# Moving the low halves of the first batch from GpSimd to VectorE, and one load up a place in the queue

## The chip, the cores and the metric

The kernel runs on one core of a Trainium2 chip. The metric is the device time of one execution in microseconds (us); lower is better. The kernel before takes 577.38 us, the median of three runs (576.22 to 577.49). The engines of the core are TensorE (PE in the rows; its weight loads are PEld), VectorE (DVE), ScalarE (ACT), GpSimd (POOL) and the sync engine (SP), whose queue issues all the loads.

## The reference

Three layers run one after the other over 4 batches of 576 positions.

```python
def _attn_ref(q, k, v):          # 8 heads of 64: four local, four strided
    scores = np.where(masks, scale * q @ k.T, -1e9)
    return softmax(scores) @ v

def _moe_ref(x, w_theta, w_tok_r, w_tok_i, w_ch):     # x: (4, 576, 512)
    theta = x @ w_theta
    zr, zi = x * np.cos(theta), x * np.sin(theta)
    y = einsum('ts,bsd->btd', w_tok_r, zr) + einsum('ts,bsd->btd', w_tok_i, zi)
    u = x + y
    return u + np.maximum(u @ w_ch, 0.0)

def _moe2_ref(x, w_gate, wq, wk, wv, wo):   # 4 experts, the top 2 are kept
    ...                                      # causal attention per expert, times wo
```

The change touches the first two layers only, and of these what belongs to batch 0, the weights, and the first load for batch 1.

## The kernel before, in words

**High and low halves.** In these two layers each operand of a large product is kept as two tiles: `hi` (the value rounded, written by ScalarE or VectorE) and `lo` (the value minus `hi`). Each product is three matmuls (`mm3`, lines 260 to 262): hi by hi, hi by lo, lo by hi. Four kinds of tiles are split so. `split_w` splits weights (line 104, or line 106 where there is a scale); the token weights `wtk` and the channel weights `wch` come through `load64`, which takes float64 input apart (lines 131 to 138). `split_act` splits the columns of `X` for theta (line 256). `rotate` splits z, the product of x with cosine and sine (line 328). In `split_w` two of three pieces have their `lo` from GpSimd, one (`c % 3 == 1`) from VectorE; in `split_act` and `rotate` the `lo` comes from GpSimd throughout this part of the program.

**The order of work.** Batch 0 goes alone at first: its attention (`attn_pair`, four pairs of heads, two local and two strided), then `theta(0, 0)`, `sines`, `rotate(0, 0)`, `theta(0, 1)`, `rotate(0, 1)`, `tokens(0, 0)` and `tokens(0, 1)` (the matmuls y). From batch 1 on, the attention of the next batch is mixed in. The program text gives priorities; a scheduler in the framework then orders the instructions of each engine by what it expects to be ready, so the diff alone doesn't tell the order.

**What orders the work near the change.** An engine executes its instructions in order. A theta tile or a y tile takes one of two PSUM buffers (`acc`, `bufs=2`), which come free when VectorE has read the theta tile twice (lines 283, 284) or added y to X (line 343). The transposes of x for `rotate` (`xn`, line 305) have one PSUM buffer, free again after VectorE's product (line 315, or 321 and 322). The raw pieces of the float64 weights go through four slots in `X[3]`, so the load of one piece (line 131) waits until VectorE has read the piece four places before (line 136). SP issues all loads in order: a load that waits holds all behind it. The tiles of batch 1's attention lie where batch 0's lay, so their first load waits for the last use there.

Of the kernel before, what the change touches and what calls it, by code (L numbers as in the profile page):

```python
# [19 lines left out]
ALU = mybir.AluOpType  # L20
# [3 lines left out]
B, S, DM, HD, NE = 4, 576, 512, 64, 4  # L24
# [23 lines left out]
def fused_kernel(ctx: ExitStack, tc: tile.TileContext, ql, kl, vl, qs, ks, vs, wth, wtk, wch, wqk, wvg, wo, out):  # L48
    nc = tc.nc

    def f(ap):
        return ap.bitcast(F32)
# [48 lines left out]
    def split_w(hi, lo, st, scale=1.0, eng=nc.gpsimd):  # L101
        nc.scalar.activation(hi, st, AF.Copy, scale=scale)
        if scale == 1.0:
            eng.tensor_tensor(lo, st, f(hi), op=ALU.subtract)
        else:
            nc.vector.scalar_tensor_tensor(lo, st, scale, f(hi), op0=ALU.mult, op1=ALU.subtract)
# [13 lines left out]
    def load64(dst, src, kt, n0, n1, scale=1.0):  # L120

        hi, lo = dst
        n = n1 - n0
        for c in range(kt):
            raw = X[3].bitcast(U16)[:, c % 4, :4 * n]
            st = X[2][:, c % 4, HALF:HALF + n]  # L130
            nc.sync.dma_start(raw[:, :4 * n - 1], src[:, c, n0:n1].bitcast(U16)[:, 1:])
            mid = raw.bitcast(U32).rearrange("p (n t) -> p n t", t=2)[:, :, 0]
            top = raw.bitcast(BF16).rearrange("p (n t) -> p n t", t=4)[:, :, 2]
            head = X[2][:, c % 4, :n]
            got = nc.scalar.copy(head.bitcast(F16).rearrange("p (n t) -> p n t", t=2)[:, :, 1], top)
            nc.vector.scalar_tensor_tensor(st.bitcast(U32), mid, 13, head.bitcast(U32), op0=ALU.logical_shift_right,
                                           op1=ALU.bitwise_or)
            split_w(hi[:, c, n0:n1], lo[:, c, n0:n1], st, scale, nc.vector if c % 3 == 1 else nc.gpsimd)
        return got.ins

    def per_tile(b, pair, g):
# [106 lines left out]
    def split_act(x, name):  # L248
        hi = act.tile([128, S], F32R, tag="ahi", name=f"{name}_hi")
        lo = act.tile([128, S], F32R, tag="alo", name=f"{name}_lo")  # L250
        if len(xsplit) == B:
            nc.scalar.copy(hi, x)
        else:
            nc.vector.tensor_copy(hi, x)  # L254
        eng = nc.vector if len(xsplit) == B and name.endswith(("0", "2")) else nc.gpsimd
        eng.tensor_tensor(lo, x, f(hi), op=ALU.subtract)  # L256
        return hi, lo

# [5 lines left out]
    def split_x(b):  # L264
        return [split_act(X[b][:, c, :], f"x{len(xsplit)}_{b}_{c}") for c in range(4)]

    sins, turns = {}, {}
    xsplit, trig, z = {}, {}, {}
# [31 lines left out]
    def rotate(b, h):  # L300
        for t in range(NT):
            w, t0, cs = TW[t], 128 * t, trig[h, t]
            xn = ps1.tile([128, 512], F32, tag="xn", bufs=1, name=f"xn_{b}_{h}_{t}")
            for c in range(2):
                nc.tensor.transpose(xn[:w, 128 * c:128 * c + 128], X[b][:, 2 * h + c, t0:t0 + w], ident)
            if t < 4:
                zf = cs
                if h == 0:
                    hi = zu.tile([128, S], F32R, tag="zuhi", name=f"zhi_{b}_{h}_{t}")
                    lo = zu.tile([128, S], F32R, tag="zulo", name=f"zlo_{b}_{h}_{t}")  # L310
                else:
                    hi = z1.tile([128, 512], F32R, tag=f"zhi{t}", name=f"zhi_{b}_{h}_{t}")
                    lo = z1.tile([128, 512], F32R, tag=f"zlo{t}", name=f"zlo_{b}_{h}_{t}")
                hi, lo = (v[:, :512].rearrange("p (a c) -> p a c", a=2) for v in (hi, lo))
                nc.vector.tensor_tensor(zf, cs, xn[:, None, :256].to_broadcast([128, 2, 256]), op=ALU.mult)
                z[h, t], z[h, 4 + t] = (hi[:, 0, :], lo[:, 0, :]), (hi[:, 1, :], lo[:, 1, :])
            else:
                zf = cs[:, 0, :]
                hi = zu.tile([128, 256], F32R, tag="z8hi", bufs=2, name=f"zhi_{b}_{h}_{t}")
                lo = zu.tile([128, 256], F32R, tag="z8lo", bufs=2, name=f"zlo_{b}_{h}_{t}")  # L320
                nc.vector.tensor_tensor(zf[0:64], xn[:64, :256], cs[:64, 0, :], op=ALU.mult)
                nc.vector.tensor_tensor(zf[64:128], xn[:64, :256], cs[:64, 1, :], op=ALU.mult)
                z[h, 8] = (hi, lo)
            if t % 2 == 0 and b > 0:
                nc.vector.tensor_copy(hi, zf)  # L325
            else:
                turns[b, h] = nc.scalar.copy(hi, zf).ins
            nc.gpsimd.tensor_tensor(lo, zf, f(hi), op=ALU.subtract)  # L328

    us = {}  # L330

# [57 lines left out]
    ain = pha.enter_context(tc.tile_pool(name="ain", bufs=3, side="right"))  # L389
# [8 lines left out]
    for b in range(B):  # L398
        angles = theta(b, 0)
        if b > 0:  # L400
            next_pair(b, 0)
            channels(b - 1)
        else:
            sines(b, 0, angles, load64(wtk_s, wtk, 9, 0, HALF))
            load_pair(1, 0, ain, 2, 2)
        rotate(b, 0)
        if b > 0:
            next_pair(b, 1)
# [375 lines left out]
```

## Time and profile before

| | us |
|---|---|
| median of 3 runs | 577.38 |
| lowest, highest | 576.22, 577.49 |
| the profiled execution: its time | 577.79 |
| the profiled execution: its span, first to last instruction | 576.0 |
| TensorE busy in the span | 535.8 (93%) |
| VectorE busy | 404.9 (70%) |
| ScalarE busy | 319.1 (55%) |
| GpSimd busy | 229.6 (40%) |

The span is 1.8 us shorter than the execution's time; that rest lies around the instructions. "Busy" counts the time in which at least one instruction of the engine executes. Matmuls are pipelined and their ends are modelled. The profile names a tile without its buffer number, and the line of the helper that issued the instruction. A row's "idle before" is the time in which the engine did nothing, with the instruction that ended the wait.

### The profile page before, as it was taken

The page shows a single profiled execution, that of the slowest core. Times are in us where ns is not written, and L with a number is a line of the kernel's source. Part 1 is how long each engine was busy: PE and PEld are TensorE (multiplying, and loading weights), DVE is VectorE, ACT ScalarE, POOL GpSimd, SP SyncE. Part 2 cuts the span into 40 slices and gives each one's busy share as a digit, 9 for nine tenths or more (in the row PEclk, how much of TensorE's full clock was granted, in tenths as well). Part 3 has the DMA queues.
Part 4 walks back from the last instruction along what each step waited for, and adds up shares of the span by engine and source line. Part 5 has one row for each costly group of instructions (what it writes and reads, how often), then busy time and mean ns, then how long its engine had stood idle before and what let it go on. Part 6 is the DMA issues. An engine that isn't in the chain of part 4 may idle for free.

```text
span 576.0 us, 12486 instructions
## 1 busy us (share of the span) xinstructions
PE 535.8 (93%) x4536; PEld 512.1 (89%) x4536; DVE 404.9 (70%) x1178; ACT 319.1 (55%) x906; POOL 229.6 (40%) x317
## 2 busy tenths in 40 slices
PE   6847879799999999999999999998999999999987
PEld 5737768799999999999999999887989999999987
DVE  4892796957686647767446553489998898888882
ACT  4882779422636216344233541267678767867873
POOL 3371283622154401355103461345444624644451
PEclk9956999799999999999999999999999999999999
DMA  9667453232320113100100010100001100100012
GB/s 279 230 212 205 136 181 107 69 96 74 105 85 22 64 32 127 33 22 23 56 1 1 1 38 19 38 2 0 2 2 52 34 1 32 42 13 12 32 42 83
DMA packets 20388, 37.52 MB, mean 65 GB/s; under 512 B 2904, under 2 KB 12296, under 8 KB 20328
## 3 DMA queue, kind: packets, MB, share of 16 engines
q1 hardware_dynamic: 20328, 36.73, 20.1%
q8 instruction: 36, 0.59, 0.4%
q14 instruction: 24, 0.20, 0.1%
HBM read 32.01 MB, written 4.72 MB: 64 GB/s over the span
## 4 chain that ended last, share of the span: by engine, by line
PE 65%; DVE 12%; ACT 6%; issue 2%; POOL 1%; POOLq 0%; DVEq 0%; ACTq 0%
PE y L260 6%; PE y L262 6%; PE y L261 6%; PE s L185 3%; PE g L262 3%; PE g L261 3%; PE g L260 3%; PE tp L616 3%; PE th L260 2%; PE av L238 2%; PE th L262 2%; PE th L261 2%; DVE nm L595 2%; PE o L572 2%; PE s L590 2%; PE pq L260 2%
## 5 line engine op out<-in xcount | busy, mean ns | idle before, releaser
L260 PE MATMUL y<-wtk_hi,zhi 128*128 128x288 f32 x288 | 86.9, 302 | 1.9 <-DVE cs L284 1.5
L262 PE MATMUL y<-wtk_hi,zlo 128*128 128x288 f32 x288 | 86.5, 301 | 0.0
L261 PE MATMUL y<-wtk_lo,zhi 128*128 128x288 f32 x288 | 86.3, 300 | 0.0
L328 POOL TENSOR_TENSOR zlo<-cs,zhi 128x512 fp32r<-128x512 f32 (+1 forms) x40 | 47.8, 1205 | 73.8 <-DVE zhi L325 44.2
L212 POOL TENSOR_TENSOR p<-p,sm 128x288 f32<-128x288 f32 (+2 forms) x48 | 29.4, 618 | 97.6 <-DVE sm L211 67.1
L613 POOL TENSOR_SCALAR p<-p,sm,gt 128x256 f32<-128x256 f32 (+1 forms) x64 | 45.3, 710 | 52.1 <-DVE sm L611 33.2
L606 ACT ACTIVATE p<-s,nm 128x128 f32<-128x128 f32 (+2 forms) x96 | 49.6, 518 | 15.0 <-DVE nm L595 7.8
L260 PEld LDWEIGHTS y<-wtk_hi,zhi 128*128 128x128 f32 x288 | 54.9, 191 | 2.5 <-DVE cs L284 1.7
L261 PEld LDWEIGHTS y<-wtk_lo,zhi 128*128 128x128 f32 x288 | 54.8, 190 | 0.2
L262 PEld LDWEIGHTS y<-wtk_hi,zlo 128*128 128x128 f32 x288 | 54.7, 190 | 0.2
L256 POOL TENSOR_TENSOR x_lo<-X,x_hi 128x576 fp32r<-128x576 f32 x24 | 36.9, 1541 | 40.8 <-DVE x_hi L254 34.4
L260 PE MATMUL th<-wth_hi,x_hi 128*128 128x256 f32 (+1 forms) x160 | 48.8, 305 | 3.2 <-ACT X L245 1.7
L185 PE MATMUL s<-k,q 128*108 128x54 f32 (+2 forms) x320 | 45.0, 286 | 4.6 <-DMA k<-in_kl 4.5
L185 PEld LDWEIGHTS s<-k,q 128*108 128x108 f32 (+1 forms) x320 | 43.0, 207 | 6.2 <-issue 6.1
L595 DVE TENSOR_REDUCE nm<-s 128x1 f32<-128x128 f32 (+2 forms) x96 | 44.3, 469 | 5.4 <-PE s L593 4.4
L261 PE MATMUL th<-wth_lo,x_hi 128*128 128x256 f32 (+1 forms) x160 | 46.6, 291 | 0.0
L262 PE MATMUL th<-wth_hi,x_lo 128*128 128x256 f32 (+1 forms) x160 | 46.5, 291 | 0.0
L260 PE MATMUL pq<-x_hi,wqk_hi 128*128 128x288 f32 x128 | 39.8, 311 | 1.0 <-DVE q L541 0.7
L285 ACT ACTIVATE cs<-cs 128x256 f32<-128x256 f32 (+1 forms) x40 | 16.7, 418 | 42.2 <-DVE cs L284 38.6
L260 PE MATMUL g<-u_hi,wch_hi 128*128 128x288 f32 x128 | 38.8, 303 | 0.0
L625 DVE TENSOR_TENSOR ptlo<-tp,pthi 128x128 fp32r<-128x128 f32 (+4 forms) x80 | 37.6, 479 | 1.2 <-ACT pthi L624 0.6
L219 ACT COPY pt<-tp 96x384 f32<-96x384 f32 (+2 forms) x44 | 20.9, 477 | 31.4 <-PE tp L215 31.3
(173 smaller groups left out, 1741.9 us busy)
## 6 DMA issues: line engine op xcount, KB each, us to landing
X<-in_wtk SPq DMA_DIRECT2D x18, 287.8 KB
q<-in_qs SPq DMA_DIRECT2D x8, 594.0 KB
q<-in_ql SPq DMA_DIRECT2D x8, 576.0 KB
v<-in_vl SPq DMA_DIRECT2D x24, 144.0 KB
out_t<-X SPq DMA_DIRECT2D x20, 128.0 KB
k<-in_kl SPq DMA_DIRECT2D x8, 304.0 KB
k<-in_ks SPq DMA_DIRECT2D x8, 288.0 KB
X<-in_wth SPq DMA_DIRECT2D x8, 255.8 KB
```

The source lines that it names most:

```text
L185: nc.tensor.matmul(s[:rm, i * kw:i * kw + w], qt[:, j0 + i, :], kt[:, k0:k0 + w], start=False, stop=i == n - 1)
L212: nc.gpsimd.tensor_tensor(tiles(p), tiles(p), each(sm), op=ALU.mult)
L219: copy(pt[:kw, :n * rm], tp[:kw, :n * rm])
L256: eng.tensor_tensor(lo, x, f(hi), op=ALU.subtract)
L260: nc.tensor.matmul(ps, ahi, bhi, start=first, stop=False)
L261: nc.tensor.matmul(ps, ahi, blo, start=False, stop=False)
L262: nc.tensor.matmul(ps, alo, bhi, start=False, stop=last)
L328: nc.gpsimd.tensor_tensor(lo, zf, f(hi), op=ALU.subtract)
L595: nc.vector.tensor_reduce(nm[:w, t + ci:t + ci + 1], s[:w, :c1 - c0], axis=AX.X, op=ALU.max, negate=True)
L606: nc.scalar.activation(p[:w, c0:c1], scs[ci][:w, :c1 - c0], AF.Exp, bias=nm[:w, t:t + 1], scale=1.0, accum_out=acc)
L613: eng.tensor_scalar(p[:w, :kn], p[:w, :kn], sm[:w, t:t + 1], gt[:w, t, e:e + 1], op0=ALU.mult, op1=ALU.mult)
L625: nc.vector.tensor_tensor(dst(ptlo), src, f(dst(pthi)), op=ALU.subtract)
```

## The change

The low halves that GpSimd computed for the weights `wtk` and `wch`, for the columns of x of batch 0 and for z of batch 0 are computed by VectorE. The first pair of batch 1's attention is asked for before the token weights instead of behind them. Below `rotate` all line numbers grow by one: line 328 before is line 329 after, 343 is 344.

```diff
@@ load64
-            split_w(hi[:, c, n0:n1], lo[:, c, n0:n1], st, scale, nc.vector if c % 3 == 1 else nc.gpsimd)
+            split_w(hi[:, c, n0:n1], lo[:, c, n0:n1], st, scale, nc.vector)
@@ split_act
-        eng = nc.vector if len(xsplit) == B and name.endswith(("0", "2")) else nc.gpsimd
+        eng = nc.vector if not xsplit or len(xsplit) == B and name.endswith(("0", "2")) else nc.gpsimd
         eng.tensor_tensor(lo, x, f(hi), op=ALU.subtract)
@@ rotate
-            nc.gpsimd.tensor_tensor(lo, zf, f(hi), op=ALU.subtract)
+            eng = nc.gpsimd if b > 0 else nc.vector
+            eng.tensor_tensor(lo, zf, f(hi), op=ALU.subtract)
@@ for b in range(B), the branch of b == 0
+            load_pair(1, 0, ain, 2, 2)
             sines(b, 0, angles, load64(wtk_s, wtk, 9, 0, HALF))
-            load_pair(1, 0, ain, 2, 2)
```

`not xsplit` holds only while no batch has been split, so for batch 0's first split. In instructions: 32 subtractions leave GpSimd for VectorE, 4 of x (128x576), 12 of `wtk` (128x288), 6 of `wch` (128x256), 8 of z (128x512) and 2 of z (128x256).

VectorE, from the products of `rotate(0, 0)` to the second tile of `theta(0, 1)` (`cs` holds the angles, then z; `xn` x transposed):

```order
 L136 SCALAR_TENSOR_TENSOR X_63<-X_64,X_63 128x288 x2
+L329 TENSOR_TENSOR zlo_0_0_771<-cs_0_0_630,zhi_0_0_770 128x512
 L315 TENSOR_TENSOR cs_0_3_681<-cs_0_3_681,xn_0_3_791 128x512
 L206 TENSOR_TENSOR p_1_2_1135<-s_1_2_1128,mx_1_2_1133 128x288
+L329 TENSOR_TENSOR zlo_0_1_779<-cs_0_1_647,zhi_0_1_778 128x512
 L283 TENSOR_SCALAR cs_1_0_821<-th_1_0_808 128x256
+L104 TENSOR_TENSOR wtk_lo<-X_63,wtk_hi 128x288
 L243 COPY X_62<-av_0_0_1053 128x384
 L104 TENSOR_TENSOR wtk_lo<-X_63,wtk_hi 128x288
 L321 TENSOR_TENSOR cs_0_4_698<-xn_0_4_799,cs_0_4_698 64x256
+L329 TENSOR_TENSOR zlo_0_2_787<-cs_0_2_664,zhi_0_2_786 128x512
```

The low halves of z and of `wtk` now stand between VectorE's reads of the theta tiles, which free TensorE's PSUM buffers.

TensorE, at the end of `theta(0, 1)` and the start of `tokens(0, 0)` (`tp`, `s`, `av` are attention of batch 1, `y` the token matmuls):

```order
 L262 MATMUL th_1_4_876<-wth_hi,x_0_3_lo 64x256
-L215 MATMUL tp_1_0_1101<-ident,p_1_0_1092 96x128 x3
+L181 LDWEIGHTS twice_89
+L181 MATMUL s_2_2_1397<-mask_s,twice_89 108x162
+L185 MATMUL s_2_2_1397<-k_2_1340,q_2_1339 108x54 x2
+L185 MATMUL s_2_2_1397<-k_2_1340,q_2_1339 108x36
+L215 MATMUL tp_1_2_1143<-ident,p_1_2_1135 96x128 x3
+L238 MATMUL av_1_0_1149<-pt_1_0_1105,v_1_0_1079 64x64 x6
+L238 MATMUL av_1_0_1149<-pt_1_1_1126,v_1_1_1081 64x64 x6
 L260 MATMUL y_0_0_1171<-wtk_hi,zhi_0_0_770 128x288
 L261 MATMUL y_0_0_1171<-wtk_lo,zhi_0_0_770 128x288
```

Attention of batch 1 that stood between the matmuls y, or behind them, now stands before the first of them.

SP, before the change, from the token weights to the first pair of batch 1 (`q_0`, `k_0`, `v_0_0`):

```order
L131 DMA X_64<-in_wtk 128x1151 x13
L157 DMA q_0_757<-in_ql 128x1152
L158 DMA k_0_758<-in_kl 128x608
L162 DMA v_0_0_761<-in_vl 96x384
L162 DMA v_0_1_763<-in_vl 96x384
L162 DMA v_0_2_765<-in_vl 96x384
L157 DMA q_1_1075<-in_ql 128x1152
```

And the same place after the change:

```order
L131 DMA X_64<-in_wtk 128x1151 x12
L157 DMA q_0_702<-in_ql 128x1152
L158 DMA k_0_703<-in_kl 128x608
L162 DMA v_0_0_706<-in_vl 96x384
L162 DMA v_0_1_708<-in_vl 96x384
L162 DMA v_0_2_710<-in_vl 96x384
L131 DMA X_64<-in_wtk 128x1151
L157 DMA q_1_1075<-in_ql 128x1152
```

One piece of the token weights of thirteen has gone behind the pair; the other twelve still stand in front. From the last tiles of `tokens(0, 1)` to the end of the program the order on every engine is what it was.

## Rows read from the trace of the kernel before

**Rows 1.** The page: TensorE's busy tenths in 40 slices of 14.4 us.
```profile
PE   6847879799999999999999999998999999999987
```
**Rows 2.** Busy time by stretch: us, then PE, PEld, DVE, ACT, POOL (instructions), PEclk, DMA share, GB/s.
```profile
65.11:85.13 20.02, 13.31 (x122) 11.65 (x120) 18.76 (x42) 17.26 (x50) 12.95 (x14) 0.91 0.57 181
85.13:107.39 22.26, 18.21 (x161) 17.25 (x161) 16.75 (x29) 16.66 (x44) 10.77 (x13) 1.00 0.24 74
107.39:114.70 7.31, 7.31 (x38) 7.20 (x39) 6.99 (x14) 3.58 (x11) 4.38 (x4) 0.53 0.40 126
133.60:330.00 196.40, 196.31 (x1797) 191.38 (x1796) 124.73 (x314) 81.27 (x179) 61.83 (x61) 1.00 0.14 46
```
**Rows 3.** Timeline of TensorE: start, us, instruction, idle time before it and its releaser.
```profile
52.82 0.43 PE L185 MATMUL s<-k,q 128*128 128x96 f32 x2 [2.75 <-DMA k<-in_kl]
...
70.28 0.69 PE L305 MATMUL xn<-ident,X 128*128 128x128 f32 x2 [2.33 <-DVE cs L315]
...
75.49 0.41 PE L305 MATMUL xn<-ident,X 128*128 128x128 f32 x2 [0.97 <-DVE cs L322]
...
85.13 0.40 PE L260 MATMUL y<-wtk_hi,zhi 128*128 128x288 f32 x1 [1.49 <-DVE cs L284]
...
100.24 0.44 PE L305 MATMUL xn<-ident,X 128*128 128x128 f32 x2 [0.93 <-DVE cs L315]
...
107.39 0.41 PE L305 MATMUL xn<-ident,X 128*64 128x128 f32 x2 [3.12 <-DVE cs L315]
```
**Rows 4.** Timeline of VectorE at 85 us and around 100 us.
```profile
85.00 1.64 DVE L136 SCALAR_TENSOR_TENSOR X<-X,X 128x288 uint32<-128x288 uint32 x1
...
99.52 0.66 DVE L315 TENSOR_TENSOR cs<-cs,xn 128x512 f32<-128x512 f32 x1
100.10 4.80 DVE L136 SCALAR_TENSOR_TENSOR X<-X,X 128x256 uint32<-128x256 uint32 x2
...
106.65 0.68 DVE L315 TENSOR_TENSOR cs<-cs,xn 128x512 f32<-128x512 f32 x1
```
**Rows 5.** Timeline of GpSimd around 100 us.
```profile
99.32 1.28 POOL L328 TENSOR_TENSOR zlo<-cs,zhi 128x512 fp32r<-128x512 f32 x1
100.55 0.74 POOL L212 TENSOR_TENSOR p<-p,sm 108x216 f32<-108x216 f32 x1
101.25 1.44 POOL L104 TENSOR_TENSOR wch_lo<-X,wch_hi 128x256 fp32r<-128x256 f32 x2
102.65 1.29 POOL L328 TENSOR_TENSOR zlo<-cs,zhi 128x512 fp32r<-128x512 f32 x1
103.89 0.72 POOL L104 TENSOR_TENSOR wch_lo<-X,wch_hi 128x256 fp32r<-128x256 f32 x1
```
**Rows 6.** Single lines, whole program: duration in ns, least/median/greatest, first and last start.
```profile
L136 DVE SCALAR_TENSOR_TENSOR X<-X,X x34: 394/450/4087, 20.5 to 106.3; 128x288 uint32<-128x288 uint32 x18, 128x256 uint32<-128x256 uint32 x16
L104 DVE TENSOR_TENSOR wtk_lo<-X,wtk_hi x6: 436/851/1036, 36.0 to 86.6; 128x288 fp32r<-128x288 f32 x6
L256 DVE TENSOR_TENSOR x_lo<-X,x_hi x8: 752/1367/1581, 319.5 to 497.0; 128x576 fp32r<-128x576 f32 x8
```
**Rows 7.** VectorE's groups in 65.11 to 85.13: count, busy us, mean ns, idle before.
```profile
L136 DVE SCALAR_TENSOR_TENSOR X<-X,X 128x288 uint32<-128x288 uint32 x9 | 8.3, 935 | 1.1 <-ACT X L135 1.1
L104 DVE TENSOR_TENSOR wtk_lo<-X,wtk_hi 128x288 fp32r<-128x288 f32 x2 | 1.8, 901 | 0.0
L206 DVE TENSOR_TENSOR p<-s,mx 128x288 f32<-128x288 f32 x2 | 0.9, 452 | 0.1
L254 DVE CAST x_hi<-X 128x576 fp32r<-128x576 f32 x1 | 0.8, 752 | 0.0
```
**Rows 8.** SP's queue: issue of the token weights and of the first pair.
```profile
27.15 15.89 SPq L131 DMA_DIRECT2D X<-in_wtk  x13
43.13 0.38 SPq L157 DMA_DIRECT2D q<-in_ql  x1
```
**Rows 9.** The loads while TensorE waits for k: the stretch, then the size of one piece (page).
```profile
43.13:52.82 9.69, 6.26 (x28) 5.90 (x29) 2.50 (x5) 1.05 (x4) 2.44 (x3) 0.66 0.94 258
X<-in_wtk SPq DMA_DIRECT2D x18, 287.8 KB
```

## The prediction

> **What bounds the kernel now.** I read the page's slices first: TensorE is at nine tenths from the ninth slice on, with dips only before and at the end [rows 1]. Then the busy time by stretch: from 133.6 to 330 us TensorE works 196.31 of 196.40 us [rows 2]. There nothing but its own work counts, and the order of all engines is unchanged. So the change is worth what it does to the time at which TensorE gets there, and that shift is then carried to the end. Between 65 and 107 us TensorE has room: it works 13.31 of 20.02 us and 18.21 of 22.26 us, while VectorE is busy 18.76 of the 20.02 [rows 2]. The timeline of TensorE says for whom it waits [rows 3]: once for the load of k (2.75 us at 52.82), else for VectorE's reads of theta tiles and its products in `rotate`, 0.93 to 3.12 us each.
>
> The longest of these is the lever. At 107.39 TensorE had waited 3.12 us for a product on VectorE that started at 106.65 [rows 3, 4]. VectorE was late because two reads of raw weights (line 136), which start at 100.10, took 4.80 us together [rows 4]. Line 136 has a median of 0.450 us; one of the two is the 4.087 of its range [rows 6]. Meanwhile GpSimd ran low halves and one scaling of p without a gap, from 99.32 to 104.61 [rows 5]. It is no better before: the nine reads in 65.11 to 85.13 have a mean of 0.935 us, twice the median [rows 7]. So VectorE's operations with two inputs in SBUF stand still while GpSimd works. The Trainium skill has this as a lock: SBUF — State Buffer, "Who interferes with whom", says that such an instruction contends with a GpSimd instruction that reads SBUF, and that the loser is blocked for the whole of the other's instruction. By that a VectorE instruction would lose one GpSimd instruction, at most 1.29 us here; the row shows that it can lose several in turn, and the measurement decides. With the rule's single instruction the 3.12 us would have been some other wait and the gain below about half.
>
> **The 32 subtractions.** By rows they cost VectorE, undisturbed: x 0.752 us (the least of line 256 there); `wtk` 0.436, taken as 0.44 (the least of line 104) [rows 6]. For z no row exists on VectorE: 512 columns lie between these two, 0.67 by the columns of x; 0.39 for the half-size ones, the least of line 136. The other end for each is what contended ones cost now: 0.851 for `wtk`, 1.367 for x (medians). I take the low end, since GpSimd, the cause of the high one, is nearly empty in these stretches after the change. It keeps only the scalings of p (0.74) and x of batch 1.
>
> *Up to the first theta.* Four x and six `wtk` add 4 × 0.75 + 6 × 0.44 = 5.6 us to VectorE, and take away GpSimd's share of its stalls of about that size. The transposes that start theta hang on p, scaled on GpSimd behind x halves that are now gone. I count this stretch as nothing, from -1 to +1.
>
> *The load of k.* SP moves one `wtk` piece of 287.8 KB behind the pair, not the token weights as a whole. At the 258 GB/s of the stretch that is 1.1 us [rows 9]. The queue also reaches q without waiting for VectorE to free the thirteenth slot. Thirteen issues take 15.89 us, 1.2 each [rows 8]; I take half of one, 0.6, since q also needs the last attention matmul of batch 0. So **-1.8 us** (0 to -2.75, where the wait is gone and TensorE's own work is next). The moved `wtk` piece belongs to the second half, wanted only behind the sines, so its delay is hidden; if not, ScalarE's read of it and z's high halves behind it are late.
>
> *65 to 85 us, the wait for the first y.* VectorE's read of the fourth theta tile ends this stretch. In the new order there stand ahead of it, more than now: four z (2.7 us) and a half-size one (0.4), seven more `wtk` (3.1), most of the ninth line 136 (0.3), one line 206 (0.45), while the cast of line 254 (0.75) goes behind: 6.2 us. Starts lie 0.08 closer than durations (0.66 us long, 0.58 to the next start [rows 4]); thirteen of these make it 5.2. Away goes the overtime: the nine line 136 have (0.935 - 0.45) × 9 = 4.4 [rows 7], of which the last, 1.64 long from 85.00 [rows 4], has 1.2 behind the point, so 3.2; two line 104 (0.901 - 0.44) × 2 = 0.9. That is 5.2 - 4.1 = 1.1, plus 0.9 for a z that waits on ScalarE and for collisions with p: **+2.0 us** (-1 to +6, the latter with the thirteen at contended durations less what stalls they have now).
>
> *Attention ahead of y.* One transposition, a score tile and the values of pair 1 that ran between or behind the matmuls y now run before the first. TensorE's total is the same and TensorE is in front of a wait there, so y starts later but has less between: 0.
>
> *85 to 115 us.* With GpSimd free of `wch` and z, the 4.80 us become 0.9. VectorE gets six `wch` and five z, about 5.5 us, but loses the stalls, 3.9 there alone, and it has longer than that: the four y tiles take TensorE some 12 us (108 matmuls at the 18.21 us / 161 of this stretch [rows 2]). So both waits, 0.93 and 3.12, go. So does what follows: after the long wait the granted clock is 0.53, that is the lower level (1.2 GHz), for 7.31 us in which TensorE works throughout [rows 2]. At the upper level (2.4 GHz) this work is 7.31 × 0.53 = 3.9 us; 3.4 are lost. Together **-7.45 us** (-9 to -3).
>
> *What is late next.* VectorE adds y to X, frees the PSUM buffer, and in the new order that stands behind `wch` and z. I put 0.5 us on the fourth y and 0.8 on the fifth, which needs the last z: **+1.3 us** (0 to 3). And the clock can fall elsewhere: a wait of 2.33 us at 70.28 was followed by transposes of 0.69 instead of 0.41 us [rows 3]. The new wait before the fifth theta tile is about as long. An even chance of half of 3.4 us: **+0.9 us** (0 to 3.4).
>
> **The sum** goes against the profiled execution, 577.79 us (span 576.0 and 1.8 around it), 0.4 above the median of 577.38: 577.8 - 1.8 + 2.0 - 7.45 + 1.3 + 0.9 = 572.75. I predict 572.8.
>
> **Rivals.**
>
> *VectorE becomes the bound (slower).* In 65 to 85 us it is busy 94%, and the change gives it more. Against: a good part of that is standing still. If the stalls have another cause than GpSimd's low halves, the fourteen added rows cost their contended time, 0.9 us for `wtk` and 1.2 for z, 12.9 us in all with no overtime saved. Then 577.8 - 1.8 + 12.9 - 7.45 = 581.5; with part of the attention hidden in it, 580.5. It decides from the point at which the added rows cost 0.8 us each on average instead of 0.45: then +2.0 becomes +7. The skill's page Perfetto Trace Analysis, "Optimizing Scalar/DVE Operations", speaks for this one: with a saturated VectorE it would move work off it, even to GpSimd. It adds that the two share a port, so that a move between them may not help. By the first half the time is the 580.5; the stalls in the trace bear out the second.
>
> *The long wait moves.* The gap at 104 to 107 is closed, but TensorE then waits 3 us before the fifth theta tile, the clock falls and y starts at the lower level: 3.4 + 2 us back, with the pair of batch 1 still held by bandwidth half of the 1.8: 577.8 - 7.45 + 2.0 + 1.3 + 3.4 - 0.9 = 576.2. For it speaks VectorE's row in 65 to 85; against it that TensorE has some attention to do in between.
>
> *All stalls gone.* GpSimd is so empty that VectorE's stretch breaks even (0 in place of +2.0), k lands in time (-2.75), no clock is lost and the new waits are small (+0.7): 577.8 - 2.75 - 7.45 + 0.7 = 568.3; with GpSimd's p in the way, 569.5.
>
> *The load does nothing*, since twelve pieces still stand in front: 572.8 + 1.8 = 574.6, within the forecast's own range.
>
> **How the numbers follow.** Forecast 0.52 (own range 570.8 to 575.4), long wait moves 0.20 (575.4 to 578), all stalls gone 0.16, slower 0.12. The measurement can't tell 0.2%, 1.15 us, from no change: 576.2 to 578.5. Faster: 0.52 + 0.16 + half of 0.20 = 0.78; same 0.10; slower 0.12. The range from 568.5 to 577.8 leaves out the slower case, a little of the moved wait and the best of the good case, some 0.18.
>
> **What would show it.** VectorE's line 136 and line 104 at 0.45 us before 107 us, with none over 1.5; x and z halves at 0.75 and 0.67; TensorE's wait for k at about 1 us; the first y at 86 to 89; no wait over 1 us and no granted clock under 0.9 from there to 120; the first theta of batch 1, now at 133.6, at about 128.5. Wrong it would be if lines 104 and 329 take 0.8 us and more on VectorE, if y starts behind 91, or if a stretch at the lower clock stands somewhere between 75 and 110.

## The result, and the profile after

The changed kernel takes 569.47 us, the median of 4 runs (567.6 to 571.74), against 576.8 (573.04 to 577.49) for four runs of the kernel before. The ratio is 0.9876, 95% interval 0.984 to 0.991: 7.3 us faster. On a second chip it was 566.59 against 576.9, ratio 0.9846 (0.978 to 0.991). The ratios, here and below, come from the single runs and not from dividing two medians; they leave out runs in the chip's slower state, and the second trace of the changed kernel below is of such a run (574.33 us). The profiled execution takes 568.58 us (span 566.8), 9.2 less than that of before.

TensorE's busy tenths and granted clock in 40 slices, from the page of the changed kernel, against [rows 1]:

```profile
PE   6859689999999999999999999998999999999987
PEclk9958879899999999999999999999999999999999
```

The timeline of TensorE after, at the points that split the span (start, us, instruction, idle time before it and its releaser), against [rows 3]:

```profile
42.46 0.58 PE L260 MATMUL th<-wth_hi,x_hi 128*128 128x256 f32 x1 [1.13 <-ACT X L245]
...
48.69 1.55 PE L185 MATMUL s<-k,q 128*128 128x96 f32 x12 [1.13 <-DMA k<-in_kl]
...
64.56 0.44 PE L305 MATMUL xn<-ident,X 128*128 128x128 f32 x2 [2.33 <-DVE cs L315]
...
83.89 0.40 PE L260 MATMUL y<-wtk_hi,zhi 128*128 128x288 f32 x1
...
105.72 0.28 PE L181 MATMUL s<-mask_s,twice 128*108 128x162 bf16 x1 [0.33 <-DVE p L206]
...
124.32 0.28 PE L260 MATMUL th<-wth_hi,x_hi 128*128 128x256 f32 x1
```

What counts is what is missing: from the first y at 83.89 to the second batch's theta at 124.32 the longest wait is 0.33 us, where 0.93 and 3.12 stood. The 2.33 us of waiting for a product of `rotate` are there as before; the wait for k is 1.13 instead of 2.75.

Busy time by stretch after (us, then PE, PEld, DVE, ACT, POOL, PEclk, DMA share, GB/s), against [rows 2]:

```profile
48.69:83.89 35.20, 28.68 (x249) 26.25 (x249) 29.60 (x84) 26.46 (x79) 5.71 (x8) 0.85 0.54 168
64.56:76.60 12.04, 9.93 (x76) 8.83 (x77) 11.58 (x32) 10.18 (x29) 0.00 (x0) 0.58 0.68 202
83.89:105.72 21.83, 21.50 (x206) 20.90 (x202) 17.72 (x46) 18.00 (x48) 2.80 (x4) 1.00 0.31 104
105.72:109.10 3.38, 3.38 (x29) 3.29 (x30) 2.57 (x10) 1.35 (x7) 1.09 (x2) 0.74 0.63 188
125.00:322.00 197.00, 196.91 (x1801) 191.97 (x1800) 125.01 (x315) 81.24 (x179) 61.85 (x61) 1.00 0.14 46
```

From 125 us on TensorE works throughout again, so what is won by then is carried to the end: the second batch's theta starts 9.27 us earlier (133.59 before) and the span is 9.2 shorter.

VectorE's lines after (ns, least/median/greatest), against [rows 6]; its nine reads of raw weights between 59.40 and 81.83 us (count, busy us, mean ns, idle before), against [rows 7]; and its reads around 96 us, against [rows 4]:

```profile
L136 DVE SCALAR_TENSOR_TENSOR X<-X,X x34: 407/444/915, 20.1 to 97.4; 128x288 uint32<-128x288 uint32 x18, 128x256 uint32<-128x256 uint32 x16
L104 DVE TENSOR_TENSOR wtk_lo<-X,wtk_hi x18: 422/448/708, 36.2 to 81.1; 128x288 fp32r<-128x288 f32 x18
L329 DVE TENSOR_TENSOR zlo<-cs,zhi x10: 415/684/692, 65.2 to 105.0; 128x512 fp32r<-128x512 f32 x8, 128x256 fp32r<-128x256 f32 x2
```

```profile
L136 DVE SCALAR_TENSOR_TENSOR X<-X,X 128x288 uint32<-128x288 uint32 x9 | 4.4, 502 | 1.1 <-ACT X L135 1.1
```

```profile
92.48 1.29 DVE L329 TENSOR_TENSOR zlo<-cs,zhi 128x512 fp32r<-128x512 f32 x2 [0.19 <-ACT zhi L327]
...
96.14 1.65 DVE L136 SCALAR_TENSOR_TENSOR X<-X,X 128x256 uint32<-128x256 uint32 x4
```

The nine reads take 4.4 us where they took 8.3, and four of the later ones 1.65 us where two took 4.80. GpSimd has these rows around that place, against the run without a gap in [rows 5]:

```profile
83.72 1.12 POOL L212 TENSOR_TENSOR p<-p,sm 108x216 f32<-108x216 f32 x2
87.70 1.44 POOL L256 TENSOR_TENSOR x_lo<-X,x_hi 128x576 fp32r<-128x576 f32 x1 [2.86 <-DVE x_hi L254]
96.04 0.46 POOL L212 TENSOR_TENSOR p<-p,sm 108x162 f32<-108x162 f32 x1 [6.91 <-PE y L262]
```

SP's queue after, against [rows 8]: twelve pieces in front of q.

```profile
26.23 14.41 SPq L131 DMA_DIRECT2D X<-in_wtk  x12
41.43 0.33 SPq L157 DMA_DIRECT2D q<-in_ql  x1
```

### The profile page after: what moved, and what is told of

It reads as the page before. It is cut to its first block, busy times and chain, and to the rows that moved or that the text cites. A ratio compares the mean times of both kernels' runs of the same rounds, so it can differ in the third digit from the quotient of the medians.

```text
span 566.8 us, 12483 instructions
## 1 busy us (share of the span) xinstructions
PE 534.0 (94%) x4536; PEld 510.2 (90%) x4536; DVE 401.9 (71%) x1210; ACT 318.2 (56%) x906; POOL 194.9 (34%) x285
## 4 chain that ended last, share of the span: by engine, by line
PE 64%; DVE 12%; ACT 4%; issue 1%; POOL 1%; POOLq 0%; DVEq 0%
PE y L260 6%; PE y L262 6%; PE y L261 6%; PE g L262 3%; PE g L261 3%; PE g L260 3%; PE s L185 3%; PE tp L617 3%; PE th L260 3%; DVE nm L596 2%; PE th L262 2%; PE th L261 2%; PE av L238 2%; PE s L591 2%; PE o L573 2%; PE tp L215 2%
## 5 line engine op out<-in xcount | busy, mean ns | idle before, releaser
L329 POOL TENSOR_TENSOR zlo<-cs,zhi 128x512 fp32r<-128x512 f32 (+1 forms) x30 | 35.8, 1205 | 55.2 <-DVE zhi L325 44.2
L256 POOL TENSOR_TENSOR x_lo<-X,x_hi 128x576 fp32r<-128x576 f32 x20 | 29.6, 1483 | 44.2 <-DVE x_hi L254 37.5
L285 ACT ACTIVATE cs<-cs 128x256 f32<-128x256 f32 (+1 forms) x40 | 16.7, 417 | 38.9 <-DVE cs L284 35.4
```

The lines of the kernel that those rows point to most:

```text
L329: eng.tensor_tensor(lo, zf, f(hi), op=ALU.subtract)
```

## The experiments

Each kernel ran beside the kernel before on the same chip. Four starts on TensorE's timeline split every trace: first theta, the first scores with the newly loaded k, first y, the second batch's first theta. In us:

| kernel | median | ratio to before (95%) | theta starts | to k's scores | to first y | to next theta | theta to theta |
|---|---|---|---|---|---|---|---|
| before | 576.8 | | 43.82 | 9.00 | 32.31 | 48.46 | 89.77 |
| before, second trace | 577.05 | | 43.74 | 7.96 | 32.33 | 47.52 | 87.81 |
| load alone | 577.41 | 1.0005 (0.997 to 1.004) | 42.55 | 8.65 | 34.16 | 47.53 | 90.34 |
| changed | 569.47 | 0.9876 (0.984 to 0.991) | 42.46 | 6.23 | 35.20 | 40.43 | 81.86 |
| changed, second trace | 566.59 | 0.9846 (0.978 to 0.991) | 45.09 | 7.32 | 35.19 | 38.87 | 81.38 |
| halves alone | 566.94 | 0.9866 (0.980 to 0.993) | 41.09 | 7.18 | 35.15 | 38.88 | 81.21 |
| z back | 569.36 | 0.9873 (0.984 to 0.990) | 43.45 | 6.58 | 31.83 | 43.63 | 82.04 |
| weights back | 574.03 | 0.9944 (0.991 to 0.998) | 44.17 | 7.06 | 32.46 | 44.41 | 83.93 |
| x back | 573.07 | 0.9938 (0.991 to 0.996) | 43.18 | 8.22 | 36.66 | 39.80 | 84.68 |
| GpSimd reads | 585.86 | 1.0117 (1.007 to 1.017) | 45.40 | 6.81 | 39.32 | 49.04 | 95.17 |
| GpSimd writes | 568.72 | 0.9853 (0.982 to 0.989) | 42.41 | 6.63 | 32.76 | 41.10 | 80.49 |
| nine pieces behind k | 568.03 | 0.9886 (0.984 to 0.993) | 37.71 | 5.30 | 41.03 | 37.62 | 83.95 |
| five pieces behind k | 571.5 | 0.9918 (0.989 to 0.995) | 39.59 | 5.92 | 34.19 | 42.71 | 82.82 |
| second half behind k | 567.73 | 0.9833 (0.979 to 0.988) | 41.75 | 6.20 | 32.02 | 40.91 | 79.13 |

The start of theta varies by 4 us between traces with one order of instructions (41.09, 42.46, 45.09), so "theta to theta" compares better than the span. The medians are of all runs, and the last four columns are of one trace each.

### Which part brings it: the load or the halves

The load alone, everything else as before:

```diff
+            load_pair(1, 0, ain, 2, 2)
             sines(b, 0, angles, load64(wtk_s, wtk, 9, 0, HALF))
-            load_pair(1, 0, ain, 2, 2)
```

> The kernel before with the pair's load moved alone; every low half stays where it was. Theory 1 (the load moves k, and the clock rises earlier because TensorE's gap is shorter): TensorE's wait for k falls from 2.75 to 1.0-1.6 us, theta then runs at the upper level about 10 us earlier, the first product of rotate comes at 60.5-61.5 instead of 65.11, and the pair of two-input reads that stood 4.8 us at 100 is still there; the time falls by 3 to 4 us, to about 573. Rival A (as the prediction had it: the wait only): first product at 63.3, time 1.8 us down, about 575. Rival B (the early gain of the changed kernel comes from the low halves that leave GpSimd, and the twelve pieces still hold the load back): first product at 64.5-65.1, time within 0.5 us of before.

Measured: no change. The order of instructions is that of the kernel before on every engine; only tile numbers differ, and one group of attention matmuls on TensorE is a place further back. The first product of `rotate` stands at 64.84 us. SP's queue in this kernel:

```profile
25.74 16.04 SPq L131 DMA_DIRECT2D X<-in_wtk  x13
41.87 0.38 SPq L157 DMA_DIRECT2D q<-in_ql  x1
```

Thirteen pieces stand in front of q, as before. VectorE in the same kernel still has its long read:

```profile
100.32 4.79 DVE L136 SCALAR_TENSOR_TENSOR X<-X,X 128x256 uint32<-128x256 uint32 x2
```

Rival B held; theory 1, which I had formed from the result, fell.

The halves alone are the changed kernel with the two load lines in their old order.

> The changed kernel with the pair's load back behind the token weights; all low halves of the first batch stay on VectorE. Theory 1: theta still starts about 1.4 us earlier (42.4), the wait for k grows back to 2.5-3 us or more and the low clock stays until about 55; the long read at 100 and the 3.12 us before the fifth tile of the second half are gone; time about 5 us below before, 572 to 573. Rival B (the halves bring the early gain too): first product at 60.0 or before, time within 1.5 us of the changed kernel, 569.5 to 571. Rival C (gain of the halves given back without the load, VectorE the bound): 575 or more.

Measured: all of the gain. This order is the changed kernel's on every engine; twelve pieces stand in front of q here too. So the load's edit did nothing, and it is the low halves that put the thirteenth piece behind the pair. Rival B came true in time (566.94, beside 566.59 for the changed kernel on that chip) and in place: the first product of `rotate` stands at 58.97. The wait for k was 2.27, less than theory 1's 2.5 to 3, and the lower clock did not last until 55.

Second traces of both kernels, unaltered:

> The kernel before unaltered, for a second trace. If the long read at 100 us is a rule of this order of instructions, one read of raw weights of over 3 us stands there again and TensorE waits about 3 us at 107; if it is chance, the reads there take under 1.5 us and the time is 573 to 574, as the lowest of the runs of before has it (573.04).

> The changed kernel unaltered, for a second trace and for a comparison on the same chip: 569.5 us, -7.3 against before; if the stretches repeat, theta starts at 42.5, the first y at 83.9 and the second batch's first theta at 124.3, each within 0.5 us.

The long read stands in all three traces of this order (before, its second trace, the load alone), so it isn't chance. VectorE and then TensorE in the second trace of before:

```profile
98.99 4.80 DVE L136 SCALAR_TENSOR_TENSOR X<-X,X 128x256 uint32<-128x256 uint32 x2
```

```profile
106.27 0.41 PE L305 MATMUL xn<-ident,X 128*64 128x128 f32 x2 [3.11 <-DVE cs L315]
```

The changed kernel's starts did not repeat within 0.5 us (theta began 2.6 us later); its stretches behind k's scores did (35.20 and 35.19, 40.43 and 38.87; the halves alone have 35.15 and 38.88), but for a piece at the lower clock in the first trace (105.72 above).

### What makes VectorE stand still

Both kernels are the changed one, with GpSimd work added at each of the 32 places from which a low half was taken. Nothing reads its results; what stands behind it on GpSimd, the scaling of p among it, comes later. The calls themselves and the arguments at `[...]` are left out here. The copy of one column in the second kernel ties the fillings to their place, and is the one small read in it.

```diff
+    def extra(hi, lo):                      # reads
+        nc.gpsimd.tensor_tensor(junk[...], f(hi), f(lo), op=ALU.subtract)
...
+    def extra(hi, lo):                      # writes
+        nc.gpsimd.tensor_copy(junk[:, :1], f(lo[...]))
+        for _ in range(2):
+            nc.gpsimd.memset(junk[...], 0.0)
```

> The changed kernel, and GpSimd makes in addition one subtraction of two inputs in SBUF for each of the 32 low parts that it used to make (same widths, x at 512 columns), into a tile that nobody reads; nothing waits for it but what stands behind it on GpSimd (scaling of p, x of the second batch). Theory P: VectorE has all its rows and stands still beside GpSimd as before the change: line 136 at a mean of 0.7 or more between 20 and 115 us, one read of over 2 us at 95 to 103, TensorE's wait for a product of rotate over 1.5 us again; time 6 to 14 us above the changed kernel, 573 to 581. Rival Q (the gain was GpSimd's queue: results come late, p waits behind them): line 136 stays at 0.46 to 0.5 with none over 1.2, TensorE's waits for p grow by 1 to 3 us, time 568 to 570, the same as with writes only.

> As the run with 32 additional subtractions, but GpSimd writes only: at each of the 32 places one copy of a single column, which ties it to the place, and two fillings of the same width with zero. Theory P: VectorE's line 136 stays at 0.46 to 0.5, none over 1.2, no wait over 1 us for a product of rotate in the second half; only what waits for p behind the fillings is later: time 0 to 2.5 us above the changed kernel, 566.6 to 569. Rival W (any work of GpSimd slows VectorE): line 136 at 0.7 or more and the time within 2 us of the run with subtractions.

Measured 585.86 and 568.72. The page's busy times and VectorE's groups between 20 and 115 us (count, busy us, mean ns, idle before), first with reads (145 is line 136, 113 is line 104, 342 is line 329 and 328 is line 315):

```profile
PE 547.4 (93%) x4536; PEld 521.2 (89%) x4536; DVE 410.9 (70%) x1210; ACT 321.9 (55%) x906; POOL 231.7 (40%) x317
...
L145 DVE SCALAR_TENSOR_TENSOR X<-X,X 128x288 uint32<-128x288 uint32 (+1 forms) x34 | 17.8, 550 | 0.8 <-ACT X L144 0.6
L113 DVE TENSOR_TENSOR wtk_lo<-X,wtk_hi 128x288 fp32r<-128x288 f32 x18 | 10.3, 599 | 0.0
L113 DVE TENSOR_TENSOR wch_lo<-X,wch_hi 128x256 fp32r<-128x256 f32 x8 | 6.0, 782 | 0.0
L342 DVE TENSOR_TENSOR zlo<-cs,zhi 128x512 fp32r<-128x512 f32 x8 | 6.4, 806 | 1.0 <-ACT zhi L340 1.0
L328 DVE TENSOR_TENSOR cs<-cs,xn 128x512 f32<-128x512 f32 x8 | 5.5, 682 | 6.1 <-ACT cs L311 4.2 <-PE xn L318 1.8
```

and with writes (144, 112, 341 and 327 are the same lines):

```profile
PE 534.6 (94%) x4536; PEld 509.9 (90%) x4536; DVE 400.7 (71%) x1210; ACT 319.5 (56%) x906; POOL 232.0 (41%) x381
...
L144 DVE SCALAR_TENSOR_TENSOR X<-X,X 128x288 uint32<-128x288 uint32 (+1 forms) x34 | 14.9, 458 | 2.8 <-ACT X L143 2.7
L112 DVE TENSOR_TENSOR wtk_lo<-X,wtk_hi 128x288 fp32r<-128x288 f32 x18 | 8.2, 470 | 0.7 <-ACT wtk_hi L110 0.7
L112 DVE TENSOR_TENSOR wch_lo<-X,wch_hi 128x256 fp32r<-128x256 f32 x8 | 3.2, 418 | 0.0
L341 DVE TENSOR_TENSOR zlo<-cs,zhi 128x512 fp32r<-128x512 f32 x8 | 5.4, 688 | 0.3 <-ACT zhi L339 0.2
L327 DVE TENSOR_TENSOR cs<-cs,xn 128x512 f32<-128x512 f32 x8 | 5.5, 686 | 4.4 <-ACT cs L310 3.6 <-PE xn L317 0.8
```

GpSimd is busy for the same time in both, 231.7 and 232.0 us; VectorE has the same 1210 instructions and needs 10.2 us more beside the reads. Its rows with two inputs in SBUF grow (`wch` from 0.418 to 0.782 us, z from 0.688 to 0.806), and the product of `rotate`, whose xn lies in PSUM so that only one input comes from SBUF, doesn't (0.686 and 0.682). So it is GpSimd's reading that costs, not its being busy, and not its queue: rivals Q and W fall.

How the 10.2 us become the difference in time is less clear. The scheduler ordered VectorE's rows differently in the two kernels, and TensorE is busy 547.4 against 534.6 us with the same 4536 matmuls, since its mean granted clock falls (0.944 and 0.971): part of the price is the clock behind the waits. Neither kernel has the changed one's order on TensorE: 216 and 215 matmuls stand between k's scores and the first y, where the changed kernel has 249.

Of theory P three things missed. Line 136 has a mean of 0.55, not 0.7 or more; the rows of `wtk` and `wch` have 0.60 and 0.78 us instead, which I put down to the additional rows running just behind a low half. No read took over 2 us: the longest has 1.45, so a row that loses several of GpSimd's in turn, as in [rows 4], is seen in the order of before alone. And the time of 585.86 is past the 581 expected at most. TensorE waits 3.42 us for a theta tile in that trace, where a wait for a product of `rotate` had been named.

The Trainium skill, SBUF — State Buffer, "Who interferes with whom", says that a VectorE instruction with two inputs in SBUF contends with a GpSimd instruction that reads SBUF and not with one that only writes it. The pair of runs agrees: 0.42 us for `wch` beside writes, 0.78 beside reads.

### Which halves

One kind at a time back on GpSimd, the other two on VectorE:

```diff
-            eng = nc.gpsimd if b > 0 else nc.vector                  # z back
+            eng = nc.gpsimd
...
-            split_w(hi[...], lo[...], st, scale, nc.vector)          # weights back
+            split_w(hi[...], lo[...], st, scale, nc.vector if c % 3 == 1 else nc.gpsimd)
...
-        eng = nc.vector if not xsplit or len(xsplit) == B and ...    # x back
+        eng = nc.vector if len(xsplit) == B and ...
```

> The changed kernel with the low parts of z back on GpSimd, ten rows; those of x and the weights stay on VectorE. Theory P (a VectorE row with two inputs in SBUF stands still while GpSimd reads SBUF): at 92 to 99 GpSimd has only the z rows of 1.3 us, not in a run of six, so a read of raw weights there takes 1.3 to 2.6 us instead of 0.41 and TensorE waits 0.5 to 2 us for a product of rotate; time 1 to 4 us above the changed kernel, 568 to 571. Rival S (VectorE's sum of work decides): VectorE loses 6.2 us of rows, first y about 2 us earlier, time 0 to 2 us below the changed kernel, 565 to 566.6.

> The changed kernel with two of three low parts of the token and channel weights back on GpSimd, 12 and 6 rows; x and z stay on VectorE. Theory P: the reads of line 136 beside them go from a mean of 0.46 to 0.6-0.7 us, the longest 1.3 to 2.5; thirteen pieces stand in front of q again and the wait for k is 1.5 to 2.5 us; time 2 to 5 us above the changed kernel, 569 to 571.5. Rival S: VectorE loses 7.8 us of rows, time at or below the changed kernel, 565 to 566.6.

> The changed kernel with the low parts of x of the first batch back on GpSimd, four rows; those of z and the weights stay on VectorE. Theory P: VectorE loses 3.0 us of rows before theta and stands still beside four GpSimd rows of 1.3-1.6 us instead; theta starts 0 to 1.5 us later against the start of the last attention, nothing changes behind it; ratio to before 0.985 to 0.989 (the changed kernel has 0.985). Rival S: VectorE, busy 10.97 of 12 us at 30 to 42, sets theta's start, so it comes 1 to 3 us earlier, ratio 0.980 to 0.983.

Measured on other chips than the changed kernel's ratios of 0.9876 and 0.9846: z back 0.9873, which the intervals don't separate from these; weights back 0.9944; x back 0.9938. These two lie above the changed kernel's on either chip, with intervals that touch its by no more than their ends, so the weights and x each bring part of the gain as far as a comparison over chips goes; for z none is shown. Whether the parts add isn't shown either: against 0.9846 the losses are 0.003, 0.010 and 0.009, together more than the 0.015 of all; against 0.9876 they are 0.000, 0.007 and 0.006, about the 0.012 of all. A kernel with one kind alone on VectorE was not run. VectorE's group of `wch` between 20 and 115 us with z back, then with the weights back:

```profile
L104 DVE TENSOR_TENSOR wch_lo<-X,wch_hi 128x256 fp32r<-128x256 f32 x8 | 5.2, 673 | 0.9 <-ACT wch_hi L102 0.9
```

```profile
L104 DVE TENSOR_TENSOR wch_lo<-X,wch_hi 128x256 fp32r<-128x256 f32 x2 | 2.2, 1118 | 0.0
```

Both kernels reach the first y sooner from k's scores (31.83 and 32.46 us against 35.2) and lose it behind (43.63 and 44.41 against 38.9 to 40.4). That is no gain and no loss of VectorE's by itself, since the attention of batch 1 went back behind the first y: 215 matmuls stand before it in both, where the changed kernel has 249. With z back, for comparison with the stretch at 48.69 above:

```profile
50.03:81.86 31.83, 26.50 (x215) 24.50 (x215) 26.67 (x69) 24.63 (x75) 10.92 (x11) 0.84 0.53 175
```

From k's scores to the next theta, which holds the same work in each, it is 75.46 us with z back and 76.87 with the weights back, against 75.63, 74.06 and 74.03 in the three traces of the changed order. Theory P held for z in time, in the longest read of raw weights (1.51 us), and in the 1.16 us that TensorE waits for a product at 100.69; since the intervals don't separate it from the changed kernel, the time can't decide against theory S there. For the weights P held in direction, in the longest read (1.70 us) and in the wait for k (2.00 us): the time went past its 571.5, to 574.03, line 136 has a mean of 0.53, not 0.6 to 0.7, and no thirteenth piece came back in front of q. Theory S fell there.

With x back both expectations failed in place and size. Theta began at 43.18, neither later nor earlier than in other traces. What is lost is lost behind it. SP's queue, then TensorE, in this kernel:

```profile
26.80 15.92 SPq L131 DMA_DIRECT2D X<-in_wtk  x13
42.81 0.38 SPq L157 DMA_DIRECT2D q<-in_ql  x1
```

```profile
51.40 1.55 PE L185 MATMUL s<-k,q 128*128 128x96 f32 x12 [3.24 <-DMA k<-in_kl]
```

The thirteenth piece is in front of q again, with the load's lines in their new place in the code. So of the three kinds it is the four low halves of x that move it, through the order that the scheduler builds, and the wait for k is 3.24 us. The granted clock then stands at 0.68 from 51.40 to 56.36 us, a stretch in which TensorE works throughout.

### Loads that do stand in front

With `issue_after`, which orders an instruction behind another one, SP issues the named loads behind the pair's k. First all nine of the first half, then the last five of these (that edit, a condition in `load64`, is left out here), then only the second half (nine stay in front):

```diff
+            with tc.issue_after(kdma[1, 0]):
+                ready = load64(wtk_s, wtk, 9, 0, HALF)
-            sines(b, 0, angles, load64(wtk_s, wtk, 9, 0, HALF))
+            sines(b, 0, angles, ready)
...
-            with tc.issue_after(sins[0, 0]):                         # second half
+            with tc.issue_after(sins[0, 0]), tc.issue_after(kdma[1, 0]):
                 ready = load64(wtk_s, wtk, 9, HALF, S)
```

> The changed kernel, and all nine pieces of the first half of the token weights are queued behind the pair's k on SP, so that the pair's load does stand in front. The two runs on the load said that its place in the code changed nothing. Theory L (VectorE and ScalarE, busy 10.97 and 11.16 of 12 us at 30 to 42, are slowed there by the pieces): q and k are issued when the last attention frees their buffer, at 36 to 39; theta starts 2 to 4 us earlier, the wait for k is gone or under 0.5; the pieces' 10 us on VectorE fall into 42 to 59, where it has 8 us free; ratio to before 0.975 to 0.980, 563 to 565. Rival M (given back): the sines stand behind the ninth piece on ScalarE, the first product of rotate is no earlier and VectorE's full stretch 59 to 82 takes the rest; ratio 0.985 to 0.992. Rival N (the pieces cost nothing where they are): theta no earlier, ratio 0.985 to 0.987.

> As the run before, but only the fifth to ninth piece stand behind the pair's k; the first four are loaded early. Theory L: half of the gain before theta and less to catch up behind it: ratio 0.978 to 0.983. Rival M: no loss behind theta here, the sines on time: better than with all nine behind, ratio 0.978 to 0.982 while that one has 0.985 or more. Rival N: 0.985 to 0.987.

> The changed kernel, and only the second half of the token weights is queued behind the pair's k on SP: nine pieces stand in front of q and k in place of twelve, and the sines, which stand behind the ninth, are not held. Theory L: three pieces fewer in VectorE's and ScalarE's full stretch before theta; theta starts about 1 us earlier (41 against 42.5), the wait for k is under 0.5 in place of 1.1 to 2.3, and the stretch from the pair's first scores to the first y keeps its 35.2 us: ratio to before 0.979 to 0.983, 564 to 566. Rival B (q waits for the buffer that the last attention of the first batch frees, not for the pieces): wait for k 0.8 to 1.5, ratio 0.983 to 0.987, the same as the changed kernel. Rival M (the pieces that are moved back fall into VectorE's full stretch before the first y): that stretch is 36.5 to 38, ratio 0.986 to 0.992.

With all nine behind k the first half of theory L holds and more: theta starts at 37.71 and the wait for k is gone. It is given back, as rival M had it, and the ratio is 0.9886. The first product of `rotate` on VectorE in that kernel, then in the changed one:

```profile
60.12 0.69 DVE L315 TENSOR_TENSOR cs<-cs,xn 128x512 f32<-128x512 f32 x1 [1.36 <-ACT cs L298]
```

```profile
59.40 0.69 DVE L315 TENSOR_TENSOR cs<-cs,xn 128x512 f32<-128x512 f32 x1 [2.23 <-ACT cs L298]
```

Theta 4.75 us earlier, the sines no earlier. With five behind k theta starts at 39.59, and the ratio of 0.9918 is no better: rival M's last clause, that it should be the better of the two, fell. Theory L's ratios, 0.975 to 0.980 and 0.978 to 0.983, fell with both. With only the second half behind k no wait for k is left, and theta to theta is 79.13, the shortest of all. Theory L's theta a us earlier (41.75 lies within what traces of one order show) and its 35.2 us to the first y (32.02, with 217 matmuls before it in place of 249) did not come true. The ratio of 0.9833 is the lowest measured, but its interval covers the changed kernel's 0.9846 and 0.9876: a version that beats the kernel before, and the changed one not demonstrably.

## Why the prediction was right or wrong

It said 572.8 within 568.5 to 577.8, faster. It was right in sign, and in the range by the first 569.47; it was 3.3 us too slow, outside its own narrower range of 570.8 to 575.4, and the second chip's 566.59 lies below both. The number is the one that the rival "all stalls gone" had (568.3 to 569.5), but not for that rival's reasons: VectorE's stretch did not break even and a wait for k was left. So the mechanism and the sign were right, the sum was too small, and that the range held is in part luck. Against the profiled execution, 577.8 to 568.6, the sum had -5.05 and the traces -9.2:

- **Up to the first theta: 0, measured -1.36.** Within traces of one order it varies by 4 us, so this 1.36 is not shown to be the change's.
- **The load of k: -1.8, measured -2.77** (9.00 to 6.23). In these two traces the wait goes from 2.75 to 1.13, where about 1 us was to be left; that the size fits so well is luck. The three traces of the order of before have waits of 2.75, 1.95 and 2.90 us, those of the changed order (the halves alone among them) 1.13, 1.51 and 2.27, and the stretch goes from 8.54 to 6.91 us on average. The reason was wrong. The step "SP moves one `wtk` piece" took the new order of SP for the work of the load's edit; the load alone moves nothing, and x back brings the thirteenth piece back. The rival that the load does nothing was right about the edit and wrong about the price, since the piece moved all the same. The other 1.15 us are TensorE's own work, 6.26 to about 5.1 us: theta got to the upper clock level at about 45.9, 3.4 us behind its start, and in the kernel before at about 49.8, 6.0 us behind it. No term had that. It is no property of the order: in the other two traces of each it comes 4.9 and 3.0 us behind theta's start after the change, 5.5 and 4.9 before it.
- **65 to 85 us: +2.0, measured +2.5** at its own point: VectorE's read of the fourth theta tile ended 19.97 us behind the start of the first product (85.08 against 65.11), now 22.43 (81.83 against 59.40). The other traces agree, 20.0 and 20.5 against 22.4 and 22.4. The step was right too: the nine reads of raw weights lost 3.9 us of overtime (8.3 to 4.4), and the prices of the rows held, 0.444, 0.448 and 0.684 us at the median for 0.45, 0.44 and 0.67. That decided against VectorE as the bound, whose point was 0.8. (The 12.9 us of that rival are more than its own prices give: seven more `wtk` at 0.9 and five z at 1.2 are 12.3 at most.)
- **Attention ahead of y: 0.** The net can't be read from the traces; what moved is large. TensorE's records from k's scores to the first y go from 212 to 249, those from there to the next theta from 409 to 376. So the stretches "to first y" (+2.9) and "to next theta" (-8.0) can only be read together.
- **85 to 115 us, what is late next and the clock: -7.45 + 1.3 + 0.9 = -5.25, measured -8.03.** The two waits went: TensorE's idle time from first y to next theta falls from 4.05 to 0.33 us. The step that was mis-sized is the one on new waits, +1.3; there are 0.33. The other 4.31 us are TensorE's work, 44.41 to 40.10. By the granted clock about 2.5 of them are the clock (7.31 us at 0.53 before, 3.38 at 0.74 after), which is what -3.4 and +0.9 had; the rest, about 1.8, is attention that had moved ahead of the first y, where no term had it. In the second trace of before and the halves alone the work is 43.20 and 38.54, of which 1.7 are clock (0.77 for 7.33 us) and some 3 attention. So the 3.4 for the clock were one trace's: the second trace of before and the load alone grant 0.77 there, not 0.53.
- **The clock elsewhere: +0.9.** A lower stretch stands behind the wait of 2.33 us in all three traces of the changed order, 12 us at 0.58, 0.58 and 0.59 (64.56 to 76.60 above). But it is not new. Behind the same wait it stands in the second trace of before and in the load alone, and is short only in the trace of before that I had read, where the upper level is back after some 3 us. Busy time as above, in the second trace of before, then in the load alone:

```profile
69.70:80.60 10.90, 10.21 (x76) 9.16 (x75) 10.38 (x27) 9.43 (x29) 9.24 (x10) 0.53 0.68 221
71.20:82.00 10.80, 9.55 (x69) 8.74 (x63) 9.87 (x27) 9.34 (x30) 9.28 (x10) 0.53 0.67 212
```

  What it costs isn't shown: after the change VectorE is busy 11.58 of the 12.04 us, TensorE 9.93. In the first trace of the changed kernel there is also 0.74 from 105.72, which the other two don't show. I had said that a lower stretch between 75 and 110 would make me wrong. By the letter that came true, with the end of the first stretch in two of the three traces and with 105.72 in one; the forecast that it stood for, no loss of clock behind the first y, failed in one trace of three.

Of the signs named, lines 104, 136 and 329, the wait for k and the missing waits came true. The first y was set at 86 to 89 and came at 83.89, the next theta at 128.5 and came at 124.32. The theta is 4.2 us early: 2.3 of them were gained by the first two stretches beyond their terms, and 2.8 behind the first y, less 0.9 lost in between.

The cause that the prediction rested on, GpSimd's reads holding up VectorE, is shown by the pair of runs with reads and writes. Not settled: what sets the moment at which theta's clock rises, and how much of the thirteenth piece's price is the wait and how much the clock behind it.

## What to carry to other kernels

Before moving work between VectorE and GpSimd, price a row undisturbed and disturbed from the trace, and ask whether the other engine's rows read SBUF: 32 subtractions cost VectorE less than the stalls that they had caused (busy 404.9 us before, 401.9 after). Where a scheduler sets the order, run or compare each edit alone before giving it a term: here one edit did nothing, and the effect forecast for it came from another. An earlier start is worth only what the next fixed point takes over: theta 4.75 us sooner was worth nothing that the runs show, as long as the sines stood where they did.

## What the runs showed of the hardware

With thirteen pieces in front of q (both traces of before, the load alone, x back) theta's matmuls behind k's scores run at the lower clock level (1.2 GHz) for about 3.4 us, in the load alone for about 6.5; in the ten traces with twelve or fewer they run at the upper one (2.4 GHz) for at least 8 us. The granted clock in the load alone, then in the changed kernel, in stretches in which TensorE works throughout:

```profile
51.20:57.70 6.50, 6.50 (x31) 6.50 (x32) 2.67 (x8) 2.03 (x10) 0.00 (x0) 0.51 0.25 73
```

```profile
48.69:59.40 10.71, 10.71 (x92) 10.54 (x93) 6.79 (x22) 6.36 (x19) 2.00 (x3) 1.00 0.53 185
```

In the load alone TensorE had stood idle for 2.90 us before it, in the changed kernel for 1.13. By the granted clock the lower level costs up to 6.50 × 0.49 = 3.2 us there (an estimate), as much again as the wait. But the wait alone does not decide it: the halves alone kept the upper level behind 2.27 us, where theta had run at it for 1.9 us before the wait, and the second trace of before had the lower one behind 1.95, where theta had run at the upper one for 0.55 us. With x back there were 1.9 us at the upper level, a wait of 3.24, and then the lower one. What does decide it stays open.

GpSimd can lose too. In the run with writes, a low half of x of the second batch took 3.40 us on GpSimd, where the same instruction 16 us earlier took 1.43 and the changed kernel's took 1.41 and 1.44:

```profile
98.56 3.40 POOL L266 TENSOR_TENSOR x_lo<-X,x_hi 128x576 fp32r<-128x576 f32 x1
```

From 98.59 to 101.96 VectorE worked there without a gap, for the most part on subtractions with two inputs in SBUF. That these held GpSimd up is inferred from their place; no run tests it by itself.
